# Order of work in the first attention round of a fused attention and gated MLP kernel

## The chip, the core and the metric

The kernel runs on one core of one Trainium2 chip. A core has TensorE (matmuls, with a second row in the profile for its weight loads), VectorE, ScalarE, GpSimd and SyncE, which issues the DMAs here. Each engine takes its instructions in the order in which the program lists them. The metric is device microseconds (us) of one execution, median of several. In the profile PE is TensorE, PEld its weight loads, DVE is VectorE, ACT is ScalarE, POOL is GpSimd and SPq the queue of SyncE.

## The reference

Eight batches, twelve heads, 448 positions, head width 64. Attention goes through a sigmoid instead of a softmax; its output is the input x of a gated MLP that mixes positions.

```python
scores = scale * np.matmul(q, k.transpose(0, 1, 3, 2)) - np.log(S)
attn = 1.0 / (1.0 + np.exp(-scores))
x = np.matmul(attn, v)                       # heads side by side: 448 x 768 for each batch
h = np.maximum(x @ w_in, 0.0)
u, v = h[..., :512], h[..., 512:]
v_n = (v - mean(v)) / np.sqrt(var(v) + 1e-06)
v_s = np.einsum('ts,bsd->btd', w_spatial, v_n) + b_spatial[None, :, None]
out = (u * v_s) @ w_out
```

## The kernel before, in words

The batches are taken two at a time, in four rounds `m` = 0 to 3. A round has these stages, and TensorE does them one after the other: attention of both batches, the v half of the MLP (`gate_values`, tiles pv), the mixing of positions of the first batch (`spatial`, pg), its u half (`gated`, pu), the mixing of the second batch, half of its u half, the output of the first batch (`output`, po), and the rest. In the rounds after the first, the attention is written out in another function (`attention`); the first has `first_attention`.

**High and low parts.** Most matmuls run on operands in a faster format, fp32r. A float32 operand is split into a high part (a cast) and a low part (the difference), and three matmuls (high·high, low·high, high·low) make one product. `split` makes both: a copy by a chosen engine, and a subtraction on VectorE (lines 107 and 108). The weights too come as raw numbers that VectorE has to convert and split.

**Attention in the first round.** `first_attention` has six sub-rounds, n = 0, 2, 4, 6, 8, 10, each for four heads. The keys are cut into three full chunks of 128 and a last one of 64. In a sub-round TensorE makes the scores of six full tiles (t = 0, 1, 2 and 4, 5, 6), and ScalarE turns each into attention values (line 277). The last keys of the four heads share one tile, the short one: `short_scores` makes its scores from the raw keys, `short_values` multiplies its attention values with v. After the six tiles' scores come their products with v (`products`), which add up in one PSUM bank, pav; the short tile's product ends that sum. In the kernel before, a sub-round begins with `short_values` of the sub-round before, then the sums leave PSUM (`attention_sums`, lines 319 to 322: one half copied by ScalarE, the other by VectorE, both subtractions on VectorE, all reading PSUM), then come `short_scores` and the six tiles. There are four PSUM tiles of two banks. In a sub-round the names y, z, w, x stand for them, the oldest first: the short scores take y, t = 0, 1, 2 take z, w, y, t = 4, 5, 6 take x, z, w, and the sum takes y again. x holds the sum of the sub-round before, so t = 4 has to wait until it is evacuated; the sum of this one has to wait until ScalarE is done with t = 2.

**Weights in portions.** `weight_steps` is a generator; `load_weights(k)` runs its next k portions. One 512-column block of w_v, w_u or w_out takes three portions: A, three integer or min/max instructions on VectorE (lines 129 to 137); B, two more (lines 139 and 142); C, the cast to the high part and the subtraction (lines 107 and 108). A block of w_sp takes one. Portion A also issues the DMA of the block two further on. The order is six blocks of w_v with four of w_sp between them, then six of w_u, then six of w_out. I number the blocks from 0: w_u5 is the last of w_u. The first round calls `load_weights` after some score tiles, six portions between attention and v half, one in the middle of each `gate_values` and one after it, and three after each step of the stages that follow.

**The v half.** `gate_values` takes the row tiles (0, 1), (2, 3), (4, 5), (6). For each group: matmuls into pv, a Relu on ScalarE to rv (line 348), on VectorE the statistics of each tile (lines 352, 353) and the subtraction of the mean (358), on GpSimd 1/sqrt(var) into rstd (355, 356), one weight portion, then for each tile the high part vn = rv·rstd (line 369, VectorE) and the low part (line 370, VectorE). Tile 3 holds rows of both batches and takes two pairs of these.

The function `in_program_order` at the end ties each engine to the order of the program text.

Of the kernel before, what the change touches and what calls it, by code (L numbers as in the profile page):

```python
# [35 lines left out]
def attn_gmlp_kernel(  # L36
# [88 lines left out]
    def convert(l, raw):  # L125

        r = raw.rearrange("p (n w) -> p w n", w=2)
        low, a = r[:, 0], r[:, 1]
        nc.vector.tensor_scalar(l, a, 0x80000000, None, op0=ALU.bitwise_and)


        af = a.bitcast(F32)
        bound = 122879.9921875
        nc.vector.tensor_scalar(
            a, a, 1, 1, op0=ALU.logical_shift_left, op1=ALU.logical_shift_right
        )
        nc.vector.tensor_scalar(af, af, bound, 2.0**-112, op0=ALU.min, op1=ALU.mult)
        yield
        nc.vector.scalar_tensor_tensor(
            l, a, 3, l, op0=ALU.logical_shift_left, op1=ALU.bitwise_or  # L140
        )
        nc.vector.scalar_tensor_tensor(
            l, low, 29, l, op0=ALU.logical_shift_right, op1=ALU.bitwise_or
        )
        yield


    AHEAD = 2
# [1 line left out]
    def weight_steps():  # L150

        steps = []
        for i in range(NCC):
            steps += [(w_v, w_v_s, i)] + [(w_sp, w_sp_s, i)] * (i < NFC)
        steps += [(w_u, w_u_s, i) for i in range(NCC)]
        steps += [(w_out, w_out_s, i) for i in range(NFC * DM // 512)]
        raws = {}

        def load(n):
            if n < len(steps):  # L160
                src, _, i = steps[n]
                w = 512 if src is w_sp else 1024

                if n < NFIRST:
                    raw = slot(tmp, f"wraw_{n}", (P, 1024), U32)[:, :w]
                else:
                    raw = work.tile([P, 1024], U32, tag="raw", name=f"wraw_{n}", bufs=4)
                raws[n] = raw.bitcast(F32) if src is w_sp else raw
                nc.sync.dma_start(raws[n], src[:, i * w : (i + 1) * w])

        for n in range(AHEAD):
            load(n)
        yield
        for n, (src, dst, i) in enumerate(steps):
            load(n + AHEAD)
            if src is w_sp and i == 0:
                nc.sync.dma_start(b_bc, b_sp.broadcast_to([P, 512]))
            hi, lo = dst[:, i, 0], dst[:, i, 1]
            val = raws.pop(n)
            if src is not w_sp:  # L180
                raw = val
                val = work.tile([P, 512], U32, tag="wval", name=f"wval_{n}", bufs=1)
                yield from convert(val, raw)
                val = val.bitcast(F32)
            split(hi, lo, val, nc.vector.tensor_copy)
            yield

# [1 line left out]
    NFIRST = NCC + NFC + 2  # L189
    BLOCK = 3  # L190

    weights = weight_steps()

    def load_weights(n):
# [29 lines left out]
    def attention_splits(b, hp):  # L224
        raw = loaded[b, hp][:, HALF:]
        s = work.tile([P, 2, 2 * S], F32R, tag="split", name=f"qks_{b}_{hp}", bufs=3)
        if b == hp == 0:

            chunk, rest, query = slice(FULL - P, FULL), slice(0, FULL - P), slice(REST, PART)
            nc.vector.tensor_copy(s[:, 0, query], raw[:, query])  # L230
            for cols in (chunk, rest):
                nc.scalar.copy(s[:, 0, cols], raw[:, cols])
            for cols in (chunk, query, rest):
                nc.vector.tensor_sub(s[:, 1, cols], raw[:, cols], s[:, 0, cols].bitcast(F32))
        else:
            scalar = b == 1 or b == 0 and hp not in (1, 2)
            split(s[:, 0, :PART], s[:, 1, :PART], raw[:, :PART], nc.scalar.copy if scalar else nc.vector.tensor_copy)
        parts_of[b, hp] = s
# [77 lines left out]
    def attention_sums(b, hp, pav):  # L316

        hi, lo = x_parts(b, hp)
        nc.scalar.copy(hi[:, 0], pav[:, 0])
        nc.vector.tensor_copy(hi[:, 1], pav[:, 1])  # L320
        for i in range(2):
            nc.vector.tensor_sub(lo[:, i], pav[:, i], hi[:, i].bitcast(F32))

    def product(ps, pairs, more=(), start=True, stop=True):
# [7 lines left out]
    def gate_values(m, ts):  # L332

        n = len(ts)
        pv = banks(f"pv_{m}_{ts[0]}")
        for i, t in enumerate(ts):
            product(
                pv[:, i, :F],
                [
                    (  # L340
                        lambda a, cc=cc, t=t: x_s[:, a, cc, t * P : (t + 1) * P],
                        lambda c, cc=cc: w_v_s[:, cc, c, :],
                    )
                    for cc in range(NCC)
                ],
            )
        rv = slot(tmp, f"rv_{m}_{ts[0]}")
        nc.scalar.activation(rv[:, :n], pv[:, :n], AF.Relu)  # L348
        mv = small.tile([P, 2, 2], F32, tag="mv", name=f"mv_{m}_{ts[0]}")
        for i in range(n):  # L350
            stats = small.tile([P, 6], F32, tag="stats", name=f"stats_{m}_{ts[i]}")
            nc.vector.bn_stats(stats, rv[:, i])  # L352
            nc.vector.bn_aggr(mv[:, i], stats)
        rstd = small.tile([P, 2], F32, tag="rstd", name=f"rstd_{m}_{ts[0]}")
        nc.gpsimd.tensor_scalar_add(rstd[:, :n], mv[:, :n, 1], 1e-6)
        nc.gpsimd.tensor_tensor(rstd[:, :n], rstd[:, :n], mhalf[:, :n], op=ALU.pow)
        for i in range(n):
            nc.vector.tensor_scalar_sub(rv[:, i], rv[:, i], mv[:, i, 0:1])
        load_weights(1)
        for i, t in enumerate(ts):  # L360
            vn = slot(big, f"vn_{m}_{t}", dtype=F32R)
            if t != NFULL:
                parts = [(vn[:, 0], vn[:, 1], slice(0, P))]
            else:

                a, c = slice(0, HALF), slice(HALF, P)
                parts = [(vn[a, 0], vn[c, 0], a), (vn[c, 1], vn[a, 1], c)]
            for hi, lo, rows in parts:
                nc.vector.tensor_scalar_mul(hi, rv[rows, i], rstd[rows, i : i + 1])
                nc.vector.scalar_tensor_tensor(  # L370
                    lo,
                    rv[rows, i],
                    rstd[rows, i : i + 1],
                    hi.bitcast(F32),
                    op0=ALU.mult,
                    op1=ALU.subtract,
                )
            vns[t] = vn
# [149 lines left out]
    def first_attention():  # L528
# [3 lines left out]
        def splits(n):  # L532
            loads(attention_splits, n)

        def short_scores(n, tag):
            shorts[n] = attention_scores(*units[n], NFULL, tag)
            loads(attention_loads, n + 4)

        def short_values(n):
            pav = attention_values(*units[n], NFULL, shorts.pop(n))  # L540
            attention_sums(*units[n], pav)

        splits(0)
        for n in range(0, end, 2):
            unit = units[n]
            full = []

            def scores(t, tag=None):
                if n == 0 and t in (1, NFULL + 1):
                    splits(1 if t == 1 else 2)  # L550
                full.append((*unit, t, attention_scores(*unit, t, tag)))
                if t == 0:
                    loads(attention_loads, n + 3)
                    loads(value_loads, n + 2)
                if t > NFULL if n == 0 else t not in (2, TILES - 1):
                    load_weights(1)

            def products(tag=None):
                for args in full:
                    attention_values(*args, tag)  # L560

            if n == 0:
                for t in FIRST:
                    scores(t)
                short_scores(n, None)
                for t in SECOND:
                    scores(t)
                splits(3)
                products()
                continue  # L570
            y, z, w, x = latest
            short_values(n - 2)
            short_scores(n, y)
            for t, tag in zip((*FIRST, *SECOND), (z, w, y, x, z, w)):
                scores(t, tag)
            splits(n + 2)
            load_weights(1)
            splits(n + 3)
            products(y)
        short_values(end - 2)  # L580

    def attention(m):

# [121 lines left out]
    for m in range(B // 2):  # L705
        if m == 0:
            first_attention()
        else:
            for _ in running:
                pass  # L710
        load_weights(2 * BLOCK)
        for ts in ((0, 1), (2, 3), (4, 5), (6,)):
            gate_values(m, ts)
            load_weights(1)
        b0, b1 = 2 * m, 2 * m + 1
        for fcs in pairs:
            spatial(b0, fcs)
# [80 lines left out]
```

## Time and profile before

| | before |
|---|---|
| time, median of 3 runs (lowest, highest) | 670.72 us (670.16, 671.21) |
| the profiled execution: time, span of its instructions | 670.48 us, 668.7 us |
| TensorE busy | 664.5 us, 99% |
| VectorE busy | 331.2 us, 50% |
| ScalarE busy | 224.8 us, 34% |
| attention of the first round on TensorE | 4.22 to 67.29 us |
| its v half, then pg, then pu | from 67.29, 95.99 and 104.78 us |

Times in the trace count from the first instruction. A row of the timeline shows start, duration, engine, line, operation, the tile written and those read, the shapes, how many instructions are merged, and in brackets how long the engine sat idle before and what ended that. The busy share of TensorE is taken from modelled ends of pipelined matmuls; whether it lost time is better read from the distance between starts of like blocks.

### The profile page before, as it was taken

The numbers are of one execution on the slowest core, as the hardware profiler recorded it, in microseconds if no ns is written. First come the engines' busy times: TensorE is split into PE (matmuls) and PEld (weight loads), VectorE is DVE, ScalarE is ACT, GpSimd is POOL, SyncE is SP. The second block draws the span as 40 slices with busy tenths as digits, with TensorE's granted clock in tenths as the row PEclk, the third lists the DMA queues.
The fourth block names the chain that finished last, engine by engine and source line by source line (L and its number), as shares of the span: only waits on it lengthen the run. The fifth ranks groups of instructions, "written<-read, shape, count | busy, mean of one in ns | idle before, by whom it ended". The sixth has DMA issues, their size and how long they took to land.

```text
span 668.7 us, 9073 instructions
## 1 busy us (share of the span) xinstructions
PE 664.5 (99%) x3866; PEld 510.4 (76%) x3866; DVE 331.2 (50%) x501; ACT 224.8 (34%) x265; POOL 19.4 (3%) x36
## 2 busy tenths in 40 slices
PE   9999999999999999999999999999999999999998
PEld 5554889999655588999964558899985556899997
DVE  5999899841357447231145644722024554653201
ACT  6877010121567510002176731010128663101112
POOL 0000010000000002000000001100000000110000
PEclk9999999999999999999999999999999999999999
DMA  8783222331445300002153430000216410000022
GB/s 299 266 270 124 63 63 67 109 111 52 163 150 168 112 1 1 0 1 82 56 182 105 163 112 1 0 1 1 82 56 197 140 60 1 0 1 1 0 83 82
DMA packets 22328, 57.34 MB, mean 86 GB/s; under 512 B 2832, under 2 KB 10128, under 8 KB 22288
## 3 DMA queue, kind: packets, MB, share of 16 engines
q1 hardware_dynamic: 22288, 56.76, 25.1%
q8 instruction: 30, 0.49, 0.3%
q14 instruction: 10, 0.08, 0.0%
HBM read 45.74 MB, written 11.01 MB: 85 GB/s over the span
## 4 chain that ended last, share of the span: by engine, by line
PE 99%; DVE 0%; issue 0%
PE pav L307 20%; PE pv L328 17%; PE pu L328 17%; PE po L328 17%; PE psc L269 14%; PE pg L328 11%; PE psc L257 3%; PE idle L701 1%; PE po_end L328 0%; DVE osb L499 0%
## 5 line engine op out<-in xcount | busy, mean ns | idle before, releaser
L277 ACT ACTIVATE at<-psc,bias_s 128x896 f32<-128x896 f32 x168 | 154.3, 1017 | 44.8 <-PE psc L269 23.5
L307 PE MATMUL pav<-at,v 128*64 128x448 f32 (+1 forms) x768 | 134.6, 545 | 0.1
L328 PE MATMUL pu<-x_s,w_u_s 128*128 128x448 f32 x576 | 117.1, 362 | 0.0
L328 PE MATMUL po<-gs,w_out_s 128*128 128x448 f32 (+1 forms) x576 | 116.2, 361 | 0.0
L328 PE MATMUL pv<-w_v_s,x_s 128*128 128x512 f32 x504 | 115.5, 390 | 0.0
L328 PEld LDWEIGHTS pu<-x_s,w_u_s 128*128 128x128 f32 x576 | 108.0, 187 | 7.2
L328 PEld LDWEIGHTS po<-gs,w_out_s 128*128 128x128 f32 x576 | 107.6, 187 | 7.1
L328 PEld LDWEIGHTS pv<-w_v_s,x_s 128*128 128x128 f32 x504 | 94.3, 188 | 22.4 <-issue 2.8
L307 PEld LDWEIGHTS pav<-at,v 128*64 128x64 f32 (+1 forms) x768 | 45.4, 135 | 77.2 <-issue 57.5
L269 PEld LDWEIGHTS psc<-qks 64*128 64x128 f32 x864 | 78.6, 185 | 24.6 <-issue 6.3
L269 PE MATMUL psc<-qks 64*128 64x448 f32 x864 | 95.2, 370 | 0.1
L107 ACT CAST gs<-g 128x896 fp32r<-128x896 f32 x16 | 15.1, 941 | 182.0 <-DVE g L431 182.0
L328 PE MATMUL pg<-w_sp_s,vn 128*128 128x448 f32 x352 | 71.7, 362 | 0.0
L328 PEld LDWEIGHTS pg<-w_sp_s,vn 128*128 128x128 f32 x352 | 66.0, 187 | 4.6
L431 DVE SCALAR_TENSOR_TENSOR g<-pu,g 128x896 f32<-128x896 f32 x16 | 17.4, 1090 | 87.2 <-PE pu L328 87.2
L107 DVE CAST qks<-raw 128x848 fp32r<-128x848 f32 x38 | 22.7, 597 | 62.7 <-PE po L328 58.7
L348 ACT ACTIVATE rv<-pv 128x1024 f32<-128x1024 f32 (+1 forms) x16 | 14.7, 921 | 108.4 <-PE pv L328 108.4
L613 DVE COPY whole<-pav 128x896 f32<-128x896 f32 x15 | 16.4, 1092 | 69.9 <-PE pav L307 69.9
L108 DVE TENSOR_TENSOR qks<-raw,qks 128x848 fp32r<-128x848 f32 x47 | 49.0, 1042 | 3.8 <-ACT qks L107 2.5
L475 ACT COPY osb<-po 128x896 f32<-128x896 f32 x23 | 20.9, 907 | 75.9 <-PE po L328 75.9
L352 DVE BATCH_NORM_STATS2 stats<-rv 128x6 f32<-128x512 f32 x28 | 19.0, 678 | 31.5 <-ACT rv L348 31.5
L408 DVE TENSOR_TENSOR g<-pg,b_bc 128x896 f32<-128x896 f32 x16 | 17.4, 1088 | 19.2 <-PE pg L328 19.2
(52 smaller groups left out, 276.9 us busy)
## 6 DMA issues: line engine op xcount, KB each, us to landing
raw<-qk_dram SPq DMA_DIRECT2D x47, 456.0 KB, 4.1
v<-v_dram SPq DMA_DIRECT2D x23, 448.0 KB, 5.6
out_dram<-osb SPq DMA_DIRECT2D x23, 448.0 KB, 2.6
wraw<-w_in_dram SPq DMA_DIRECT2D x12, 512.0 KB, 4.8
wraw<-w_out_dram SPq DMA_DIRECT2D x6, 512.0 KB, 3.5
last<-qk_dram SPq DMA_DIRECT2D x3, 448.0 KB, 4.7
wraw<-w_sp_dram SPq DMA_DIRECT2D x4, 256.0 KB, 4.3
raw<-qk_dram SPq DMA_DIRECT2D x1, 296.0 KB, 2.9
```

What stands on the lines that cost most here:

```text
L107: copy(hi, src)
L108: nc.vector.tensor_sub(lo, src, hi.bitcast(F32))
L257: nc.tensor.matmul(psc[odd * HALF : (odd + 1) * HALF, j, :S], key[rows], query[rows], start=True, stop=True,)
L269: nc.tensor.matmul(psc[:, j, :S], s[rows, a, k : k + P], s[rows, e, REST:PART], start=i == 0, stop=i == len(TERMS) - 1,)
L277: nc.scalar.activation(at, psc[:, :, :S], AF.Sigmoid, bias=bias_s, scale=QK)
L307: nc.tensor.matmul(pav[heads, odd, :S], vt[rows, t, heads], at[rows, j], start=start, stop=stop)
L328: nc.tensor.matmul(ps, st, mv, start=start and i == 0, stop=stop and i == len(ops) - 1)
L352: nc.vector.bn_stats(stats, rv[:, i])
L408: nc.vector.tensor_add(g, pg[:, :, :S], bb)
L431: nc.vector.scalar_tensor_tensor(g, pu[:, :, :S], 0.0, g, op0=ALU.max, op1=ALU.mult)
L475: nc.scalar.copy(osb, whole_of.pop(es)[:, :, :S])
L613: copy(whole, pav)
```

## The change

1. In sub-rounds 2 to 10 of `first_attention`, `short_scores` comes ahead of `short_values`. VectorE copies the finished sums in one piece from PSUM to an SBUF tile, `whole`; behind the sigmoid of t = 2 ScalarE casts the high part of x from it and VectorE subtracts. The tile takes the SBUF slot of the short attention values. The last sums (n = 10) still leave by `attention_sums`, with the subtractions in the other order.
2. The portion after the splits in sub-rounds 2 to 10 is gone (five portions); one comes behind the last sums, and `gate_values` is followed by two portions instead of one (four more).
3. From the end of the first attention on, a converted block's high part is cast by ScalarE, issued in portion B; C has only the subtraction.
4. In `gate_values`, of all four rounds, ScalarE multiplies rv by rstd for the high part; VectorE keeps the low part.
5. The second split of the first batch (hp = 1) is made in two pieces, the columns of the first needed chunk and of the queries ahead.

```diff
@@ convert: its last yield goes
-        yield
@@ weight_steps
                 val = val.bitcast(F32)
+                apart = bool(late)
+                if apart:
+                    nc.scalar.copy(hi, val)
+                yield
+                if apart:
+                    nc.vector.tensor_sub(lo, val, hi.bitcast(F32))
+                    yield
+                    continue
             split(hi, lo, val, nc.vector.tensor_copy)
             yield
@@ attention_splits
+        elif b == 0 and hp == 1:
+
+            for cols in (slice(FULL - P, PART), slice(0, FULL - P)):
+                split(s[:, 0, cols], s[:, 1, cols], raw[:, cols], nc.vector.tensor_copy)
@@ attention_sums
-        for i in range(2):
+        for i in (1, 0):
@@ gate_values
-                nc.vector.tensor_scalar_mul(hi, rv[rows, i], rstd[rows, i : i + 1])
+                nc.scalar.mul(hi, rv[rows, i], rstd[rows, i : i + 1])
@@ first_attention
         def short_scores(n, tag):
-            shorts[n] = attention_scores(*units[n], NFULL, tag)
+            at = attention_scores(*units[n], NFULL, tag)
+            shorts[n] = big.pop(), at
             loads(attention_loads, n + 4)

         def short_values(n):
-            pav = attention_values(*units[n], NFULL, shorts.pop(n))
-            attention_sums(*units[n], pav)
+            tag, at = shorts.pop(n)
+            return tag, attention_values(*units[n], NFULL, at)
...
             y, z, w, x = latest
-            short_values(n - 2)
             short_scores(n, y)
+            tag, pav = short_values(n - 2)
+            big.append(tag)
+            whole = work.tile([P, 2, 512], F32, tag=tag, name=f"whole_{n}", bufs=1)[:, :, :S]
+            nc.vector.tensor_copy(whole, pav)
             for t, tag in zip((*FIRST, *SECOND), (z, w, y, x, z, w)):
                 scores(t, tag)
+                if t == NFULL - 1:
+                    split(*x_parts(*units[n - 2]), whole, nc.scalar.copy)
             splits(n + 2)
-            load_weights(1)
             splits(n + 3)
             products(y)
-        short_values(end - 2)
+        tag, pav = short_values(end - 2)
+        big.append(tag)
+        attention_sums(*units[end - 2], pav)
+        load_weights(1)
@@ the loop over m
+        late.append(m)
         load_weights(2 * BLOCK)
         for ts in ((0, 1), (2, 3), (4, 5), (6,)):
             gate_values(m, ts)
-            load_weights(1)
+            load_weights(2)
```

More of the change, by code (lines that the diff above doesn't have):

```diff
@@ L190, in attn_gmlp_kernel @@
     BLOCK = 3
+    late = []
     weights = weight_steps()
```

## The prediction

> **What bounds the kernel now.** I read the page first, then the timeline of TensorE.
>
> ```profile
> span 668.7 us, 9073 instructions
> PE 664.5 (99%) x3866; PEld 510.4 (76%) x3866; DVE 331.2 (50%) x501; ACT 224.8 (34%) x265; POOL 19.4 (3%) x36
> PE 99%; DVE 0%; issue 0%
> ```
>
> TensorE is the whole chain of waits. So an edit gains only where TensorE's blocks stand further apart than they need to, and loses wherever another engine makes TensorE wait. The same page's average hides where the second can happen. The busy times by stretch (PE, PEld, DVE, ACT, POOL, then clock and DMA) show it:
>
> ```profile
> 40.00:50.00 10.00, 10.00 (x76) 4.94 (x74) 9.16 (x17) 8.14 (x11) 0.00 (x0) 1.00 0.86 284
> 70.00:80.00 10.00, 10.00 (x46) 8.28 (x45) 9.48 (x21) 1.03 (x1) 0.60 (x2) 1.00 0.36 105
> ```
>
> VectorE is at 92 to 95% in the two stages that the change rearranges, ScalarE at 81% in the first and 10% in the second.
>
> How far apart are the blocks? The timeline of TensorE, first round (psc is scores, pav the products with v), then a later round:
>
> ```profile
> 16.36 3.98 PE L269 MATMUL psc<-qks 64*128 64x448 f32 x36
> 20.35 5.64 PE L307 MATMUL pav<-at,v 128*64 128x448 f32 x32
> 26.67 3.99 PE L269 MATMUL psc<-qks 64*128 64x448 f32 x36
> 57.73 4.05 PE L269 MATMUL psc<-qks 64*128 64x448 f32 x36
> 61.72 5.64 PE L307 MATMUL pav<-at,v 128*64 128x448 f32 x32
> 183.20 3.87 PE L269 MATMUL psc<-qks 64*128 64x448 f32 x36
> 187.00 4.73 PE L307 MATMUL pav<-at,v 128*64 128x448 f32 x24
> ```
>
> The same 36 score matmuls take 187.00 − 183.20 = 3.80 us there and 20.35 − 16.36 = 3.99 in sub-round 2. That is all the first round can win.
>
> **Part 1, the sub-rounds.** From 16.36 to 57.73 are four sub-rounds, 41.37 us. Dense they would take 3.80 for the scores and 26.67 − 20.35 = 6.32 for the rest, 4 × 10.12 = 40.48; the fifth block has 61.72 − 57.73 − 3.80 = 0.19 to win. Sum 1.08 us. Does the new order reach 3.80? The later round already has it: short scores, short values, a copy of the sums on VectorE, then the tiles.
>
> ```profile
> 183.39 1.09 DVE L613 COPY whole<-pav 128x896 f32<-128x896 f32 x1 [7.40 <-PE pav L307]
> 184.11 4.60 ACT L277 ACTIVATE at<-psc,bias_s 128x896 f32<-128x896 f32 x5 [0.35 <-PE psc L269]
> ```
>
> ScalarE's casts, grouped by shape (busy us, mean ns of one):
>
> ```profile
> L107 ACT CAST qks<-raw 128x848 fp32r<-128x848 f32 x9 | 7.9, 940 | 1.0 <-DMA raw<-qk_dram 1.0
> L232 ACT CAST qks<-raw 128x256 fp32r<-128x256 f32 x1 | 0.4, 404 | 0.1
> L232 ACT CAST qks<-raw 128x128 fp32r<-128x128 f32 x1 | 0.3, 297 | 1.5 <-DMA raw<-qk_dram 1.5
> ```
>
> The copy ends 184.48, 1.28 us after the block's start; t = 4 wants its bank after three tiles, 1.9 us. ScalarE's sigmoids follow each other at about 0.9 us, so t = 2 ends at 184.11 + 2 × 0.9 + 1.0 = 186.92, just ahead of pav at 187.00. The added cast of the high part (0.94, by the 128x848 cast) goes behind t = 2; ScalarE's total for the sub-round is 7 × 0.9 + 3 × 0.94 = 9.1 of 10.1 us, so it stays covered. VectorE gives away one portion and exchanges a half copy and two half subtractions for a whole copy of 1.09 and one subtraction. Where its splits run late, they delay the copy; 1.9 − 1.28 = 0.6 us in hand covers that. I take 1.08, bounds 0 and 1.08.
>
> The two-piece split: at the start TensorE waits for the low part of one split,
>
> ```profile
> 8.23 1.50 PEld L269 LDWEIGHTS psc<-qks 64*128 64x128 f32 x16 [0.16 <-DVE qks L108]
> ```
>
> and the first piece is ready earlier by more than that: at most 0.16 us. So the v half begins some 1.2 us earlier (bounds 0 and 1.2).
>
> **Parts 2 to 4, the v half.** Five portions now fall between the last sums and the pu matmuls, while casts and vn products leave VectorE. By amounts it is even. The rows of VectorE, ScalarE and GpSimd:
>
> ```profile
> 67.43 0.53 ACT L319 CAST x_s<-pav 128x448 fp32r<-128x448 f32 x1 [3.07 <-PE pav L307]
> 68.54 1.14 DVE L322 TENSOR_TENSOR x_s<-pav,x_s 128x448 fp32r<-128x448 f32 x2
> 69.60 0.42 DVE L129 TENSOR_SCALAR wval<-wraw 128x512 uint32<-128x512 uint32 x1
> 70.98 0.69 DVE L139 SCALAR_TENSOR_TENSOR wval<-wraw,wval 128x512 uint32<-128x512 uint32 x1
> 72.43 0.43 DVE L107 CAST w_u_s<-wval 128x512 fp32r<-128x512 f32 x1
> 72.89 0.69 DVE L108 TENSOR_TENSOR w_u_s<-wval,w_u_s 128x512 fp32r<-128x512 f32 x1
> 73.62 0.43 DVE L129 TENSOR_SCALAR wval<-wraw 128x512 uint32<-128x512 uint32 x1
> 77.53 0.69 DVE L352 BATCH_NORM_STATS2 stats<-rv 128x6 f32<-128x512 f32 x1
> 81.17 0.48 DVE L369 TENSOR_SCALAR vn<-rv,rstd 128x512 fp32r<-128x512 f32 x1
> 81.69 0.75 DVE L370 SCALAR_TENSOR_TENSOR vn<-rv,rstd,vn 128x512 fp32r<-128x512 f32 x1
> 85.01 0.69 DVE L352 BATCH_NORM_STATS2 stats<-rv 128x6 f32<-128x512 f32 x1
> 87.25 0.81 POOL L356 TENSOR_TENSOR rstd<-rstd,mhalf 128x2 f32<-128x2 f32 x1
> 100.04 0.69 DVE L108 TENSOR_TENSOR w_u_s<-wval,w_u_s 128x512 fp32r<-128x512 f32 x1
> 100.65 0.68 DVE L352 BATCH_NORM_STATS2 stats<-rv 128x6 f32<-128x512 f32 x1
> 101.59 0.49 DVE L358 TENSOR_SCALAR rv<-rv,mv 128x512 f32<-128x512 f32 x1
> 75.79 1.03 ACT L348 ACTIVATE rv<-pv 128x1024 f32<-128x1024 f32 x1 [7.82 <-PE pv L328]
> 96.23 0.60 ACT L348 ACTIVATE rv<-pv 128x512 f32<-128x512 f32 x1 [3.10 <-PE pv L328]
> ```
>
> A takes 70.98 − 69.60 = 1.38 us, B 72.43 − 70.98 = 1.45, C 73.62 − 72.43 = 1.19. Moved in: B, C of w_u0 and A, B, C of w_u1, 1.45 + 1.19 + 4.02 = 6.7 us. Moved out: the casts of w_u1 to w_u5, 5 × 0.46 (72.89 − 72.43) = 2.3, and eight vn products, 8 × 0.52 (81.69 − 81.17) = 4.2. So 0.2 us more work. Each moved A takes its DMA along, past nothing but loads that are issued anyway:
>
> ```profile
> wraw<-w_in_dram SPq DMA_DIRECT2D x12, 512.0 KB, 4.8
> ```
>
> A block lands 4.8 us after its issue and is wanted two blocks, 8 us of portions, later. Nothing.
>
> What isn't even is the order. **The queue of ScalarE** matters: portion B of w_u3 is issued behind the group (0, 1), ahead of the Relu of the group (2, 3). Its cast waits for VectorE's B; that Relu stands behind the cast; and VectorE's next instruction, the statistics, waits for the Relu. Before, the Relu waited for TensorE alone and was done when VectorE came. Now each group has a round trip that VectorE spends idle. I call S the start of a group's statistics.
>
> The unseen prices are the 512-column cast and product on ScalarE. By the slope of its two smaller casts above, 107 ns for 128 columns, 512 columns take 404 + 214 = 618 ns; bounds 0.40 and 0.94. The Relu of 512 columns took 0.60, so I take 0.62 for both, and 0.04 for a hand-over.
>
> - The first S. The last sums start at 67.43 − 1.2 = 66.23, VectorE is through with them 2.17 later (69.60 − 67.43) at 68.40. Then B, C of w_u0 (issued too early for ScalarE's cast), A, B of w_u1, its cast on ScalarE (0.70 with hand-overs), its subtraction 0.69, A, B of w_u2: 68.40 + 2.64 + 2.83 + 0.70 + 0.69 + 2.75 = 78.0. The cast of w_u2 and the Relu: 0.62 + 1.03 − 0.11 (neighbours on ScalarE overlap so much) + three hand-overs = 1.62. S = 79.6; before it was 77.53.
> - One group. rstd is ready at S + 3.04 (87.25 + 0.81 − 85.01), by which time VectorE is through with the mean and a subtraction of weights; the product on ScalarE to S + 3.74; two low parts 1.42 (0.75 each, the second starting a little ahead of the first's end); A, B 2.75; cast and Relu 1.62. Sum 9.53. The group with tile 3 has one low part more, 10.2; the third's trip has the short Relu, 9.1. The last S = 79.6 + 28.8 = 108.4; before 100.65.
> - w_u5. Its subtraction stands behind the last group's statistics and mean: 108.4 + 1.43 (101.59 + 0.49 − 100.65) + 0.6 = 110.4. Before it ended at 100.73.
>
> Who waits for it?
>
> ```profile
> 95.99 8.96 PE L328 MATMUL pg<-w_sp_s,vn 128*128 128x448 f32 x44
> 104.78 14.56 PE L328 MATMUL pu<-x_s,w_u_s 128*128 128x448 f32 x72
> 119.18 8.96 PE L328 MATMUL pg<-w_sp_s,vn 128*128 128x448 f32 x44
> ```
>
> A pu product takes 18 matmuls at (119.18 − 104.78)/72 = 0.20 us; the 17th reads w_u5's low part, so at 104.78 + 3.2 = 108.0, and 106.8 if all is 1.2 earlier. There were 7.3 us in hand; now w_u5 comes 3.6 us late. TensorE stands at its first pu product. The pg block ahead of it is covered: tile 3 is complete at 79.6 + 9.5 + 3.74 + 2.1 = 95.0 and wanted at 94.8 + 1.8.
>
> Behind it, VectorE comes to its sums of pg some 5 us after w_u5, at about 115; they free banks that TensorE wants from 118 on, and later blocks of w_out have a cast less on VectorE each, so I add nothing. The same vn product in rounds 2 to 4 has VectorE mostly idle around it and 7 us between Relus on ScalarE: nothing, unless w_u5's kind of wait exists there, and no weights are left by then.
>
> Net: −1.2 + 3.6 = +2.4 us. On the profiled execution's 668.7 span and the 1.8 around it, 670.48 becomes 672.9; the median stands 0.24 above that execution, so **673.1 us**. The bounds: about eight ScalarE steps are in the chain; at 0.40 each 1.8 us less, at 0.94 each 2.6 more: 671.3 to 675.7.
>
> **The rivals.**
> - *Work decides, not order.* If VectorE's queue after the last sums is as early as its amount of work says (0.2 us more than before), w_u5 is there before 106.8, and 670.72 − 1.2 = 669.5 remains. For it: 7.3 us in hand. Against: three trips of 1.6, and four waits for rstd and product. It decides from 3.6 us less chain on; the lower price of ScalarE gives half of that. Chance 0.16.
> - *Half a stall.* Quicker hand-overs and ScalarE steps near their lower bound leave 1 to 2.2 us of it: 670.5 to 671.8, no difference that can be told. Chance 0.18.
> - *A stall with a slow clock behind it.* At the start the first 18 score matmuls, behind an idle TensorE, took longer than dense ones:
>
> ```profile
> 4.22 2.83 PE L269 MATMUL psc<-qks 64*128 64x448 f32 x18
> ```
>
> 2.75 to the next block against 3.80/2. A stall can bring that back, 0.9 us, and it is likelier with a longer one: 5 us of stall gives 670.72 − 1.2 + 5 + 0.9 = 675.4. Against: the row's 0.9 has low parts' waits in it. Chance 0.11. The Trainium skill (TensorE: Matmul & The Clock Gate, "What's actually happening") says that the array falls to half its clock after an idle window of about 3.4 us, whose place is free. By it 3.6 us would seldom hold a whole window; an estimate from the page for one that does is 1.7 us more. Only a run with such a gap could show it; the trace before has none.
> - *The first round wins nothing*, because the copy comes late: everything starts 1.2 later, 674.3. Counted with the forecast.
>
> **How the numbers follow.** Forecast 0.55, the rivals 0.16, 0.18, 0.11. The range takes in the first rival's point and the upper bound of the forecast: 669.4 to 675.6. A difference under 0.2%, 1.34 us, can't be told from none. Faster (below 669.4) is a good half of the first rival, 0.10; the same is its other part, the half stall and a little of the forecast's low edge, 0.26; slower 0.64. For the likeliest case alone 671.8 to 674.8.
>
> **What would show it.** The first round: score blocks 3.80 apart from pav, v half starting about 66.1. The v half: ScalarE's Relus no longer released by TensorE but behind casts, VectorE idle before the statistics with ScalarE as the cause, the last w_u subtraction near 110, and a gap in TensorE's pu block after some 15 matmuls with VectorE's w_u as releaser. The forecast is wrong if pu has no gap, or if the gap is at another block.

## The result

The changed kernel takes 675.83 us (median, 675.4 to 676.75) against 670.72 us (670.16 to 671.21). The ratio is 1.008, 95% interval 1.007 to 1.0091: slower by 5.1 us, where 2.4 were forecast; the range ended at 675.6.

The page of the changed kernel:

```profile
span 673.4 us, 9062 instructions
PE 665.3 (99%) x3866; PEld 512.1 (76%) x3866; DVE 314.4 (47%) x455; ACT 254.6 (38%) x308; POOL 17.8 (3%) x36
PE 93%; DVE 5%; ACT 1%; issue 0%; ACTq 0%
L340 PE MATMUL pu<-x_s,w_u_s 128*128 128x448 f32 x576 | 119.3, 366 | 4.0 <-DVE w_u_s L189 2.1
```

The span is 4.7 us longer. VectorE lost 17 us of busy time and ScalarE gained 30, yet now 5% of the chain of waits lies on VectorE, and the pu matmuls, which never waited before, wait for the weights w_u. The timeline of TensorE has the place (columns as before):

```profile
9.60 4.73 PE L319 MATMUL pav<-at,v 128*64 128x448 f32 x24
26.09 3.87 PE L281 MATMUL psc<-qks 64*128 64x448 f32 x36
29.90 4.73 PE L319 MATMUL pav<-at,v 128*64 128x448 f32 x24
65.88 28.86 PE L340 MATMUL pv<-w_v_s,x_s 128*128 128x512 f32 x126
103.38 3.16 PE L340 MATMUL pu<-x_s,w_u_s 128*128 128x448 f32 x15
108.41 0.47 PE L340 MATMUL pu<-x_s,w_u_s 128*128 128x448 f32 x1 [1.87 <-ACT w_u_s L186]
110.98 13.06 PE L340 MATMUL pu<-x_s,w_u_s 128*128 128x448 f32 x56 [2.09 <-DVE w_u_s L189]
123.88 8.96 PE L340 MATMUL pg<-w_sp_s,vn 128*128 128x448 f32 x44
```

The account in three terms. The v half begins at 65.88 instead of 67.29: −1.4. The 17th pu matmul starts at 110.98 where 103.38 + 3.2 = 106.6 was due: +4.4. And the last 56 take 123.88 − 110.98 = 12.9 us where 56 × 0.20 = 11.2 was due: +1.7. Sum 4.7. From 123.88 on, the blocks have the lengths they had before.

The last term is a slow clock. The busy times by stretch (columns as in the prediction; the number behind the five engines is the granted clock, 1.00 at full speed):

```profile
106.00:109.00 3.00, 1.01 (x4) 0.35 (x2) 1.75 (x4) 1.12 (x2) 0.00 (x0) 1.00 0.10 15
109.00:112.00 3.00, 1.02 (x3) 0.94 (x4) 1.85 (x4) 0.60 (x1) 1.32 (x2) 0.84 0.44 160
112.00:115.00 3.00, 3.00 (x11) 2.68 (x10) 2.71 (x6) 0.12 (x1) 0.00 (x0) 0.59 0.00 0
115.00:118.00 3.00, 3.00 (x17) 2.81 (x16) 2.93 (x5) 0.62 (x1) 0.00 (x0) 1.00 0.42 117
```

In the third row TensorE has 11 matmuls, in the fourth, at full clock, 17. The second and third row lack 3 × 0.16 + 3 × 0.41 = 1.7 us of full clock, which is the whole term. Before, no stretch of this stage was below 1.00.

And the round trips, on ScalarE and VectorE (L186 is the weight cast, L360 the Relu, L364 the statistics, L189 the subtraction of w_u):

```profile
78.01 0.62 ACT L186 CAST w_u_s<-wval 128x512 fp32r<-128x512 f32 x1 [3.60 <-DVE wval L142]
78.54 1.02 ACT L360 ACTIVATE rv<-pv 128x1024 f32<-128x1024 f32 x1
```

```profile
79.59 0.69 DVE L364 BATCH_NORM_STATS2 stats<-rv 128x6 f32<-128x512 f32 x1 [1.61 <-ACT rv L360]
89.16 0.69 DVE L364 BATCH_NORM_STATS2 stats<-rv 128x6 f32<-128x512 f32 x1 [1.62 <-ACT rv L360]
108.89 0.69 DVE L364 BATCH_NORM_STATS2 stats<-rv 128x6 f32<-128x512 f32 x1 [1.18 <-ACT rv L360]
110.24 0.68 DVE L189 TENSOR_TENSOR w_u_s<-wval,w_u_s 128x512 fp32r<-128x512 f32 x1
```

Before, VectorE came to each of these statistics with the Relu done. Now it sits idle for 1.6 us, three times (the third at 99.75, not shown), and 1.2 the fourth, behind a cast and a Relu each time. The first group's Relu starts at 78.54; before it started at 75.79, released by TensorE.

### The profile page after: what moved, and what is told of

Read it like the earlier page. It is cut to its first block, busy times and chain, and to the rows that moved or that the text cites. A ratio compares the mean times of both kernels' runs of the same rounds, so it can differ in the third digit from the quotient of the medians.

```text
span 673.4 us, 9062 instructions
## 1 busy us (share of the span) xinstructions
PE 665.3 (99%) x3866; PEld 512.1 (76%) x3866; DVE 314.4 (47%) x455; ACT 254.6 (38%) x308; POOL 17.8 (3%) x36
## 4 chain that ended last, share of the span: by engine, by line
PE 93%; DVE 5%; ACT 1%; issue 0%; ACTq 0%
PE pav L319 19%; PE po L340 17%; PE pu L340 17%; PE psc L281 14%; PE pv L340 13%; PE pg L340 9%; PE psc L269 3%; DVE vn L382 1%; DVE stats L364 1%; DVE wval L142 1%; DVE wval L139 1%; ACT rv L360 1%; PE idle L721 0%; DVE w_u_s L189 0%; DVE rv L370 0%
## 5 line engine op out<-in xcount | busy, mean ns | idle before, releaser
L340 PE MATMUL pu<-x_s,w_u_s 128*128 128x448 f32 x576 | 119.3, 366 | 4.0 <-DVE w_u_s L189 2.1
L107 DVE CAST qks<-raw 128x848 fp32r<-128x848 f32 (+2 forms) x39 | 22.8, 585 | 60.4 <-PE po L340 56.6
L108 DVE TENSOR_TENSOR qks<-raw,qks 128x848 fp32r<-128x848 f32 (+2 forms) x48 | 48.7, 1022 | 1.3
L381 ACT ACTIVATE vn<-rv,rstd 128x512 fp32r<-128x512 f32 (+1 forms) x32 | 21.8, 718 | 47.3 <-POOL rstd L368 37.9
L364 DVE BATCH_NORM_STATS2 stats<-rv 128x6 f32<-128x512 f32 x28 | 19.0, 679 | 40.4 <-ACT rv L360 40.4
L382 DVE SCALAR_TENSOR_TENSOR vn<-rv,rstd,vn 128x512 fp32r<-128x512 f32 (+1 forms) x32 | 23.3, 749 | 20.6 <-ACT vn L381 20.3
```

The source lines that it names most:

```text
L107: copy(hi, src)
L108: nc.vector.tensor_sub(lo, src, hi.bitcast(F32))
L340: nc.tensor.matmul(ps, st, mv, start=start and i == 0, stop=stop and i == len(ops) - 1)
L381: nc.scalar.mul(hi, rv[rows, i], rstd[rows, i : i + 1])
L382: nc.vector.scalar_tensor_tensor(lo, rv[rows, i], rstd[rows, i : i + 1], hi.bitcast(F32), op0=ALU.mult, op1=ALU.subtract,)
```

## The experiments

Unless said otherwise each is the changed kernel with one edit, timed beside the kernel before; a ratio is to that kernel, with its 95% interval. L numbers are those of each kernel.

**Relus ahead of the casts.** The order of ScalarE's queue alone is changed; VectorE keeps its order and its work.

```diff
-    def gate_values(m, ts):
+    def gate_values(m, ts, portions):
         nc.scalar.activation(rv[:, :n], pv[:, :n], AF.Relu)
+        load_weights(portions)
...
-        load_weights(2 * BLOCK)
+        load_weights(2 * BLOCK - 2)
         for ts in ((0, 1), (2, 3), (4, 5), (6,)):
-            gate_values(m, ts)
-            load_weights(2)
+            gate_values(m, ts, 2)
+        load_weights(2)
```

> The changed kernel with one thing else: in the first v half ScalarE gets each group's Relu ahead of the weight cast that it stood behind; VectorE's order stays. Theory (round trips over ScalarE's queue): four trips of 1.6 us go, w_u5's low part ends near 104.4 instead of 110.9 and TensorE wants it at 106.6: no gap in the pu block, clock 1.0, 669.3 us (the first round's 1.4 us is kept). Rival (VectorE simply has too much work ahead of pu): VectorE has the same work, so w_u5 stays near 110 and the time near 675.8. Rival (the vn products on ScalarE are late): gap shrinks by little, above 673.

Measured 669.47 us (668.94 to 670.08); ratio to before 0.9983, 0.9974 to 0.9992. Its timelines of TensorE, ScalarE and VectorE:

```profile
65.74 28.88 PE L340 MATMUL pv<-w_v_s,x_s 128*128 128x512 f32 x126
103.25 14.56 PE L340 MATMUL pu<-x_s,w_u_s 128*128 128x448 f32 x72
```

```profile
82.41 1.03 ACT L360 ACTIVATE rv<-pv 128x1024 f32<-128x1024 f32 x1 [0.26 <-PE pv L340]
85.74 0.62 ACT L186 CAST w_u_s<-wval 128x512 fp32r<-128x512 f32 x1 [2.30 <-DVE wval L142]
```

```profile
85.62 0.69 DVE L365 BATCH_NORM_STATS2 stats<-rv 128x6 f32<-128x512 f32 x1
103.73 0.68 DVE L189 TENSOR_TENSOR w_u_s<-wval,w_u_s 128x512 fp32r<-128x512 f32 x1
```

The second group's Relu, shown here, is released by TensorE again, and the next cast runs while VectorE takes the statistics. VectorE has no idle time ahead of any of the four statistics; its waits for the products, 0.76 us ahead of the low parts of each of the first three groups, are still there. w_u5 ends at 104.4, ahead of 103.25 + 3.2, and pu has no gap. The trips are the cause of the stall, and this version is faster than both kernels, though than the kernel before by only 1.3 us.

**Casts back on VectorE**: in `weight_steps`

```diff
-                apart = bool(late)
+                apart = False
```

> The changed kernel with all weight casts on VectorE; the vn products stay on ScalarE, the portions stay moved. Theory of the round trips: VectorE has 2.3 us more work but no trips; w_u5 ends near 104.8, no gap, 669.3 us. Rival (too much work on VectorE): w_u5 at 110.9 + 2.3 = 113.2, a gap of 6.6 us, 678 us.

669.6 us (668.83 to 669.84), ratio 0.9984 (0.9975 to 0.9994). 

```profile
103.88 14.56 PE L340 MATMUL pu<-x_s,w_u_s 128*128 128x448 f32 x72
```

```profile
104.64 0.69 DVE L108 TENSOR_TENSOR w_u_s<-wval,w_u_s 128x512 fp32r<-128x512 f32 x1
```

There is more work on VectorE, and w_u5 is done 5.6 us earlier (105.3 against 110.9). The amount was not the cause.

**Products back on VectorE**: in `gate_values`

```diff
-                nc.scalar.mul(hi, rv[rows, i], rstd[rows, i : i + 1])
+                nc.vector.tensor_scalar_mul(hi, rv[rows, i], rstd[rows, i : i + 1])
```

> The changed kernel with the vn products on VectorE; the weight casts stay on ScalarE. Theory of the round trips: the four trips stay, VectorE takes over products that it waited for anyway: w_u5 near 112, gap 5.5 us, slow clock behind it, 677 us. Rival (the products on ScalarE cost the time): gap gone, 669.3 us.

678.16 us (676.9 to 678.52), ratio 1.011 (1.0095 to 1.0125).

```profile
109.98 0.47 PE L340 MATMUL pu<-x_s,w_u_s 128*128 128x448 f32 x1 [3.15 <-ACT w_u_s L186]
112.55 14.24 PE L340 MATMUL pu<-x_s,w_u_s 128*128 128x448 f32 x56 [2.10 <-DVE w_u_s L189]
```

The trips stay and w_u5 ends at 112.5. That is 1.6 us later than in the changed kernel, 1.3 counted from the start of the v half: the products on ScalarE helped by this much, though VectorE gave away 4.2 us of work for it. The slow clock is longer here. The next block starts at 126.62, so the last 56 matmuls take 14.07 us, 2.9 more than dense ones, and the clock is still low where it was full again in the changed kernel:

```profile
115.00:118.00 3.00, 3.00 (x10) 2.66 (x9) 2.90 (x6) 0.62 (x1) 0.00 (x0) 0.50 0.05 8
```

**Both back on VectorE**, the two edits together; what remains is the first round and the moved portions.

> The changed kernel with neither casts nor products on ScalarE, so that only the moved portions and the first round's new order are left. Theory of the round trips: VectorE has 6.7 us more work than before and no trips; w_u5 near 107.5, a gap of about 0.9 us, too short for a slow clock: 670.2 us, well below the changed kernel although VectorE does more. Rival (work decides): 110.9 + 2.3 + 4.2 = 117, a gap of 10 us, 681 us.

671.44 us (671.04 to 672.06), ratio 1.0013 (1.0003 to 1.0023).

```profile
104.13 3.61 PE L340 MATMUL pu<-x_s,w_u_s 128*128 128x448 f32 x16
108.00 11.48 PE L340 MATMUL pu<-x_s,w_u_s 128*128 128x448 f32 x56 [0.26 <-DVE w_u_s L108]
119.31 8.96 PE L340 MATMUL pg<-w_sp_s,vn 128*128 128x448 f32 x44
135.31 1.97 PE L340 MATMUL po<-gs,w_out_s 128*128 128x448 f32 x9
138.34 12.78 PE L340 MATMUL po<-gs,w_out_s 128*128 128x448 f32 x62 [0.26 <-DVE w_out_s L108]
150.96 7.36 PE L340 MATMUL pu<-x_s,w_u_s 128*128 128x448 f32 x36
```

w_u5 ends at 107.9 as worked out, and pu loses 119.31 − 104.13 − 14.4 = 0.8. What was not expected: the output block behind it waits too, for w_out, and takes 15.65 us instead of 14.4; with this the time comes out 1.2 us above the 670.2 expected. VectorE's lateness is handed on to the next weights. Yet this kernel, with 6.5 us more on VectorE in the v half (2.3 of casts and 4.2 of products), beats the changed one by 4.4 us.

**Filling the gap.** Is the slow clock a clock, and the gap its cause? Here 22 matmuls, and in further runs 16, 14 and 11, are put ahead of the first pu product, into the bank that it starts anew.

```diff
         pu = banks(f"pu_{b}_{fcs[0]}")
+        for _ in range(22 if b == 0 and fcs[0] == 0 else 0):
+            nc.tensor.matmul(pu[:, 0, :S], w_v_s[:, 0, 0, :P], x_s[:, 0, 0, :S], start=True, stop=True)
```

> The changed kernel with 22 matmuls of 0.2 us ahead of the first pu product, into the bank that this product then starts anew; they fill TensorE's gap of 4.4 us and move nothing else. Theory (1.7 us of the loss are matmuls at half clock behind the gap): pu runs at 0.20 us a matmul from the first on, 674.1 us. Rival (the slow matmuls come from something else in that stretch, VectorE's or DMA traffic): still 0.37 us each, 675.8 us or more.

673.99 us (673.51 to 674.14).

```profile
107.93 14.61 PE L340 MATMUL pu<-x_s,w_u_s 128*128 128x448 f32 x72
122.37 8.96 PE L340 MATMUL pg<-w_sp_s,vn 128*128 128x448 f32 x44
```

There are 72 matmuls in 14.44 us, 0.20 each: the 1.8 us below the changed kernel are the clock's. The stall itself is only filled, not removed.

> The same with 11 such matmuls: TensorE idles some 2.2 us instead of 4.4 and goes on at the same point. If an idle stretch of over 3 us is needed for the slow clock: 0.20 us a matmul behind it, 674.1 us. If 2.2 us are enough: 675.8 us.

675.69 us as median of four, and they differ: three at 675.5 to 676.1 with a mean clock of 0.997, one at 674.2 with 1.000. The profiled one is of the three (timeline, and stretch):

```profile
111.04 13.05 PE L340 MATMUL pu<-x_s,w_u_s 128*128 128x448 f32 x56 [2.01 <-DVE w_u_s L189]
111.00:114.00 3.00, 2.96 (x8) 2.66 (x9) 1.72 (x4) 0.72 (x1) 0.43 (x1) 0.54 0.00 1
```

So 2.0 us of idle time can be enough. By the mean clock of the fourth execution they aren't always, if its gap was as long; only the profiled one shows its gap. The two shorter gaps have one execution each:

> The changed kernel with 16 filling matmuls: TensorE idles about 1.0 us ahead of the 17th pu matmul. With 2.0 us idle (11 filling matmuls) the next 3.4 us ran at 0.37 us a matmul, with 0.3 us (another variant) at 0.20. If an idle microsecond is enough: 0.37 us behind it; else 0.20 us and about 674 us.

> The same with 14 filling matmuls, about 1.4 us idle: 0.37 us a matmul behind the gap if the bound lies below that, else 0.20 us.

674.38 and 673.84 us; the timeline rows are of the 16 and the 14, the stretch of the 14:

```profile
111.46 11.47 PE L340 MATMUL pu<-x_s,w_u_s 128*128 128x448 f32 x56 [1.01 <-DVE w_u_s L189]
```

```profile
111.02 11.47 PE L340 MATMUL pu<-x_s,w_u_s 128*128 128x448 f32 x56 [1.39 <-DVE w_u_s L189]
111.00:114.00 3.00, 2.98 (x15) 2.80 (x16) 1.73 (x4) 0.73 (x1) 0.40 (x1) 1.00 0.00 0
```

In these two executions, with 1.0 and 1.4 us, the clock stayed. In the stretch from 111 the kernels with 11 and 14 matmuls have nearly the same work on VectorE, ScalarE and DMA; only the clock, 0.54 against 1.00, sets 8 matmuls apart from 15. The other engines' work and the DMA traffic are not the cause.

**The first round alone**: casts and products as in the two edits above, and the portions where the kernel before has them.

```diff
             splits(n + 2)
+            load_weights(1)
             splits(n + 3)
...
         attention_sums(*units[end - 2], pav)
-        load_weights(1)
...
             gate_values(m, ts)
-            load_weights(2)
+            load_weights(1)
```

> Only the first round's part of the change: new order, copy of the sums, split in two pieces; the portions stay where the kernel before has them, casts and products on VectorE. Theory: the sub-rounds' score blocks are dense at about 3.8 us (VectorE's extra portion finds room) and the v half begins 1.0 to 1.4 us earlier, w_u5 near 99.4: no gap, 669.3 us. Rival (the portions have to go for the order to work): the copy of the sums is late behind the portion, t = 4 waits, the v half begins less than 0.5 us earlier, 670.3 us.

670.22 us (669.81 to 670.57), ratio 0.9993 (0.9984 to 1.0003): no difference that can be told. TensorE's timeline, and what its weight loads waited for in the sub-rounds (us, times, longest):

```profile
47.21 4.26 PE L281 MATMUL psc<-qks 64*128 64x448 f32 x36
51.40 4.73 PE L319 MATMUL pav<-at,v 128*64 128x448 f32 x24
67.20 28.88 PE L340 MATMUL pv<-w_v_s,x_s 128*128 128x512 f32 x126
```

```profile
PEld psc L281 <- DVE whole L589: 1.3, 4, 0.5
```

My theory fell here, and the rival held. The score block shown takes 51.40 − 47.21 = 4.19 us, the longest of the five; they take 20.0 in all, against 19.1 in the changed kernel and 20.1 in the kernel before. With the fifth portion in the sub-round VectorE comes late to the copy of the sums, and t = 4 waits for its bank.

**The portions out, the old order in.** The kernel with the Relus ahead, and in `first_attention` the text of the kernel before (short values first, `attention_sums`), without its portion.

> The kernel with the Relus ahead of the casts (669.5 us) with the sub-rounds' old order put back: short values first, the sums leaving PSUM in four pieces; the portions stay moved out of the sub-rounds. With the new order and the old portions the v half began at 67.2 us, with both new at 65.9. Theory (order and portions are both needed): score blocks stay near 3.99, since ScalarE's chain from the short sigmoid is unchanged; v half near 67, 670.4 us. Rival (relief of VectorE alone does it): blocks near 3.8, v half near 66, 669.5 us.

670.57 us (670.0 to 672.41), ratio 1.0 (0.9991 to 1.001).

```profile
47.44 4.00 PE L281 MATMUL psc<-qks 64*128 64x448 f32 x36
51.42 5.64 PE L319 MATMUL pav<-at,v 128*64 128x448 f32 x32
67.30 28.85 PE L340 MATMUL pv<-w_v_s,x_s 128*128 128x512 f32 x126
```

3.98 a block. Taking the first pav block's start as origin, since the start-up before it differs from execution to execution, the v half begins 57.25 us later in the kernel before, 57.20 with the new order alone, 57.10 with the portions out alone, and 56.28 with both (56.27 to 56.29 in all nine kernels here that have both). Neither part gains by itself.

**The order alone**, in the kernel before, one execution: the sums leave PSUM in four pieces.

```diff
-            short_values(n - 2)
             short_scores(n, y)
+            short_values(n - 2)
```

> The kernel before with only the order of short scores and short values exchanged; the sums leave PSUM by both engines as before. Theory (ScalarE's chain from the short sigmoid to t = 2 sets the score block): the block falls from 3.99 to about 3.8 us, v half about 0.9 us earlier. Rival (the evacuation of the sums into four pieces sets it): the block stays above 3.95.

677.3 us. Two timeline rows of one sub-round:

```profile
27.78 1.01 ACT L277 ACTIVATE at<-psc,bias_s 128x896 f32<-128x896 f32 x1 [3.17 <-PE pav L307]
31.07 2.08 PE L269 MATMUL psc<-qks 64*128 64x448 f32 x18 [1.35 <-DVE x_s L322]
```

The theory missed. The rival's bound held and the wait is for the sums, as it says, but neither foresaw that the block would grow, from 3.99 to 5.50 us (27.58 to 33.08). The short sigmoid waits for the product of the short tile before, whose SBUF slot comes round to it; ScalarE's half of the sums stands behind that sigmoid, VectorE's behind ScalarE's, and t = 4 waits 1.35 us for them. The changed kernel gives the short tile a slot of its own and copies the sums by one engine, and there the new order has no such wait; which of the two it needs was not tested apart.

**Late casts on ScalarE in the kernel before**, with its portions unmoved (the edit of `weight_steps` and `convert`, and `late`).

> The kernel before with only the late weight casts on ScalarE, portions unmoved. Theory of the round trips: the trips are there too, three of about 1.6 us, but w_u5 had 7.3 us in hand: later low part, no gap, 670.7 us. Rival (these casts on ScalarE cost time by themselves): a gap ahead of pu, over 672 us.

671.0 us (670.61 to 671.34), ratio 1.0003 (0.9993 to 1.0013).

```profile
87.32 0.70 DVE L360 BATCH_NORM_STATS2 stats<-rv 128x6 f32<-128x512 f32 x1 [1.61 <-ACT rv L356]
101.53 0.69 DVE L189 TENSOR_TENSOR w_u_s<-wval,w_u_s 128x512 fp32r<-128x512 f32 x1
```

There is no gap, as expected, but only one full trip and not three. A Relu stands behind three of the casts, but only at 87.32 do VectorE's statistics come straight behind the portion B. Ahead of the first group the subtraction C stands between (waits of 0.69 us for the cast and 0.23 for the Relu), ahead of the last the vn work does, and VectorE doesn't wait. w_u5 ends at 102.2 instead of 100.7, well inside its slack.

## Why the prediction was wrong

The direction, the place and the mechanism of the stall held; the size did not, because a second cost behind the stall was left out of the sum. The time lies 0.23 us outside the range.

- *The step that failed* is "Net: −1.2 + 3.6 = +2.4 us". It has no term for a slow clock, which it left to a rival at 0.11, with 5 us of stall as its condition. The slow clock came in all five executions of the changed kernel (mean clock 0.994 to 0.997), and in the profiled one behind two idle stretches of 1.87 and 2.09 us with one matmul between. There it cost 1.7. The row that I priced it by gave 0.9 and was read wrongly: the granted clock of the kernel before is 1.00 in that stretch too (4 to 8 us), so those 0.9 us are no slow clock. The estimate worked out from the Trainium skill (TensorE: Matmul & The Clock Gate, "What's actually happening") was 1.7 and agrees. The condition that the Trainium skill gives there, an idle window of about 3.4 us, does not: with 11 filling matmuls 2.0 us were enough in the profiled execution, and the measurement decides.
- *The stall*, 3.6 forecast, measured 4.4. The chain itself was nearly right: first statistics 79.6 (79.59), groups of 9.53 (9.57), 10.2 (10.59) and 9.1 (9.14), w_u5 at 110.4 (110.92). The 0.4 in the group of tile 3 is its third low part, which added 1.0 us where 0.7 was taken. The product on ScalarE took 0.72, not 0.62; the cast took 0.62. Besides, TensorE arrived 0.2 us earlier. That the first statistics agree to 0.01 is luck in part: the terms given for the 1.62 of cast and Relu add up to 1.66, and VectorE was through with the last sums at 68.32, not 68.40.
- *The first round*: 1.2 forecast, 1.41 in the profiled executions. 0.97 of it is in the sub-rounds, where 1.08 was worked out; the blocks take 3.81 against 3.80. The rest is start-up and not shown to be the change's: kernels that share this first round begin their first pav block anywhere from 9.45 to 10.35 us, the kernel before at 10.04. What the two-piece split gains can't be told in that.
- *"VectorE gives away one portion"* was treated as a relief that the order didn't need. It needs it: without it the gain is gone (the first round alone).
- *"Work decides, not order"*: shown wrong. With the casts back on VectorE there is more work and no gap.
- *The range* was to take in the forecast's upper bound, 675.7, but ends at 675.6; the time lies above both.
- *"I add nothing" for w_out*: right for the changed kernel; with both back on VectorE that margin was used up and cost 1.25 us.

## What to carry to other kernels

When work is handed from a busy engine to an idle one, write down what stands behind it in the idle engine's queue, and whether the busy engine waits for that: here a 0.6 us cast ahead of a Relu cost the engine that it was to relieve 1.6 us a time, and putting the Relu ahead turned 675.8 us into 669.5. A slack is used up by the sum of moved work and new waits, so follow each late result to its reader, and then the reader's own lateness onwards. Price a stall of TensorE that comes near 2 us with the slow clock behind it, here 1.7 us and with a longer stall 2.9.

## What was not expected of the hardware

With gaps of 1.01 and 1.39 us TensorE went on at 0.20 us a matmul. With 2.0 us the profiled execution showed some 3.4 us at 0.37 us a matmul (clock 0.50), a cost of about 1.7, and two of the three others have its mean clock. Behind 1.87 and 2.09 us with one matmul between, the mean clock was low in every execution, in two of them 0.994 and 0.995 instead of 0.997. With 3.15 and 2.10 us (the products back on VectorE) the mean clock was 0.994, and the low clock lasted some 6.8 us, twice as long; the two unprofiled executions at 0.994 and 0.995 may be of that kind, which is not shown. Whether there is a bound between 1.4 and 2.0 us, and what decides at 2.0, stays open: the shorter gaps have one execution each.

The start differs as well between kernels with the same first round. TensorE's first score blocks with the Relus ahead, and with both back on VectorE:

```profile
4.23 2.36 PE L281 MATMUL psc<-qks 64*128 64x448 f32 x18
```

```profile
4.23 3.26 PE L281 MATMUL psc<-qks 64*128 64x448 f32 x18
```

The same 18 matmuls from the same start take 0.9 us more in one execution than in the other. The granted clock is 1.00 in both, so it is not the slow clock; the cause stays open. That alone moves the start of the v half, and a gain of a few tenths in this stretch can't be read from one profile.
